# Attention and a gated FFN in one kernel: the second group's units visited two at a time

## The chip, the cores and the metric

The kernel runs on one core of a Trainium2 chip. The metric is the device time of one execution in microseconds. Before the change the median of three runs is 683.46 us (681.92 to 683.64).

## The reference

```python
# q, k, v: 4 batches x 12 heads x 448 tokens x 64, float32
scores = scale * q @ k.T ; upper triangle masked ; attn = softmax(scores)
x = (attn @ v), heads side by side: 1792 tokens x 768
rms = sqrt(mean(x * x) + 1e-6) ; xn = x / rms * rms_g
g = xn @ w_gate ; val = xn @ w_val          # 768 x 1536 each
out = (g * sigmoid(g) * val) @ w_out        # 1536 x 768
```

## The kernel before, in words

**Groups and units.** The tokens are worked in three groups. Groups 0 and 1 hold the first 256 queries of two batches each, group 2 all other queries. Within a group attention is cut into units: a pair of heads of one batch and some of its queries. `UNITS` lists them, `ENDS` = [12, 24, 60] is where each group ends, and `DP` = 3 is the distance in units by which scores run ahead. Units of groups 0 and 1 have `kind` 0: 256 queries in two blocks, 128 queries by 128 keys and 128 queries by 256 keys. Those of group 2 have kind 1 (128 queries, 384 keys) or kind 2 (64 queries of two batches, 448 keys).

**Steps of a unit.** `steps_s(p)` makes the scores of unit p on TensorE (one half e = 0, 1 for each head). VectorE masks and reduces them out of PSUM (L202), ScalarE takes the exponential one slot later (L205), and `norm` (posted seven slots later for kind 0) takes a reciprocal on VectorE (L214) and scales, for units 10 to 23 on ScalarE (L208). `steps_t(p)` gives two steps, one for each e: three transposes on TensorE into a bank and a copy `pt` out of it, for units 12 to 23 on ScalarE (L255). `steps_a(p)` multiplies the copies with v (L275) into a half of one bank and copies the result out (L292, on ScalarE for group 1). The banks of PSUM: `m` two, `s` two, and one each of `t`, `x`, `y` and `a`. Scores of a unit take the two `s` banks; for every second unit of the third group they take `x` and `y`. Transposes of e = 0 go to `t`, those of e = 1 to `x` as far as unit 24, and to `t` after it.

**Order.** It is written out by hand: all engines get their instructions in program order from one Python loop. While group 0's attention runs by itself at first, with a little of the FFN, from then on the FFN of one group runs with the attention of the next beneath it. The FFN of a group is a list of 36 weight units (24 of the gate and value weights, 12 of the output weights); one unit is 18 matmuls of 512 columns, 6 in each of 3 **slots**. After the six matmuls of a slot the loop (L916 to L940) puts in the steps of attention that are due, spread evenly from slot `HOLD` to slot `AT` of the block, then splits and conversions of later weights, and `tick()` runs what was posted with a delay for that slot. So `post(7, f)` means that f's instructions stand at the end of the seventh slot, counted from the one that posts.

```python
while done < goal and (done - at) < (goal - at) * (i - HOLD[w_]) / (AT[w_] - HOLD[w_]):
    steps[done]()
    done += 1
```

In that first block VectorE and ScalarE also convert the 64-bit weights (L414 to L419), split each weight into two parts (L429, L431) and evict every FFN bank (L492 to L505, or L486 in the output part).

**The list of steps.** `round_steps(p)` makes the rounds of groups 0 and 1. For group 1 a round is three steps: `both` (scores of unit p + 3, products of unit p), then the two steps of transposes of unit p + 1. `refill()` stands ahead of group 1's first round: scores of units 12, 13 and 14 and the transposes of unit 12, with empty steps between. `round_of_two(p)` makes the rounds of group 2, four steps for two units: `last` (the last transposes of unit p + 1, then `visit`: loads of v, scores of p + 3 and p + 4, products of p and p + 1, the two copies), and then the transposes of p + 2 (two steps) and the first of p + 3.

Of the kernel before, what the change touches and what calls it, by code (L numbers as in the profile page):

```python
# [34 lines left out]
UNITS = [(g, kind, c, k, NP * (first + k) + c, base + QUERIES[kind] * k)  # L35
         for g, parts in enumerate(GROUPS) for c in range(NP)
         for kind, n, first, base in parts for k in range(n)]
LAST = {(g, c): max(i for i, u in enumerate(UNITS) if u[0] == g and u[2] == c)
        for g in range(NG) for c in range(NP)}
ENDS = [max(i for i, u in enumerate(UNITS) if u[0] == g) + 1 for g in range(NG)]  # L40
# [11 lines left out]
WARM = [9, 0, 0, 2]  # L52
EXTRA = 4
AT = [108, 73]
HOLD = [9, 0]
XT = 768
HX = XT // 2
RING = 6
DP = 3
# [3 lines left out]
def attention_ffn(ctx: ExitStack, tc: tile.TileContext, qk0, qk1, qk2, v, v2, w, g, out, out2):  # L63
# [11 lines left out]
    def pool(name, bufs, at=ctx, **kw):  # L75
        return at.enter_context(tc.tile_pool(name=name, bufs=bufs, **kw))
# [3 lines left out]
    ps = pool("ps", 1, space=PSUM)  # L80
# [13 lines left out]
    def bank(tag, bufs=1):  # L94


        return ps.tile([P, W], F32, tag=tag, name=tag + "_ps", bufs=bufs)
# [34 lines left out]
    def post(delay, fn):  # L132
        if delay <= 0:
            fn()
        else:
            later.setdefault(now[0] + delay, []).append(fn)
# [32 lines left out]
    def blocks(kind):  # L169

        return [(0, P), (P, 2 * P)] if kind == 0 else [(0, KEYS[kind])]

    def steps_s(p):


        if not 0 <= p < len(UNITS):
            return []
        _, kind, _, _, _, _ = UNITS[p]
        pr = hs[p] = dict(norms=[])
        bl = blocks(kind)  # L180
        nb = 2 * len(bl)

        def scores(pss):
            for i, (o, wd) in enumerate(bl):
                for h in range(1 + (kind == 2)):
                    for e in range(2):
                        r = raw_qk[p][e * D: (e + 1) * D, h]
                        if kind == 2:
                            ps, q0, nq = pss[e][h * D: (h + 1) * D, :wd], 0, D
                        else:  # L190
                            ps, q0, nq = pss[e][:, o: o + wd], i * P, P
                        k0 = nq if kind else 2 * P
                        nc.tensor.matmul(ps, r[:, q0: q0 + nq], r[:, k0: k0 + wd],  # L193
                                         start=True, stop=True)

        def softmax(e, i, pss):
            o, wd = bl[i]
            ps, sp = pss[e][:, o: o + wd], pr["sp"][e][:, o: o + wd]
            n = len(bl) * e + i
            nm, sm, rs = (pr[m][:, n: n + 1] for m in ("nm", "sm", "rs"))  # L200
            mk = mask2 if kind == 2 else mask[:, 3 * P - wd:]
            nc.vector.tensor_tensor_reduce(  # L202
                out=sp, in0=ps, in1=mk, scale=nsc, scalar=3.0e38,
                op0=ALU.add, op1=ALU.min, accum_out=nm)
            post(T["exp" if p >= ENDS[0] else "exp0"], lambda: nc.scalar.activation(  # L205
                sp, sp, AF.Exp, bias=nm, scale=-1.0, accum_out=sm))
            if ENDS[0] - 2 <= p < ENDS[1]:
                pr["norms"].append(lambda: nc.scalar.mul(sp, sp, rs))  # L208
            else:
                pr["norms"].append(lambda: nc.gpsimd.tensor_scalar(  # L210
                    sp, sp, rs, 1.0, op0=ALU.mult, op1=ALU.mult))

        def norm():
            nc.vector.reciprocal(pr["rs"][:, :nb], pr["sm"][:, :nb])  # L214
            post(2 if ENDS[0] - 2 <= p < ENDS[0] else 0, lambda: [f() for f in pr["norms"]])

        def step():
            for nm in ("nm", "sm", "rs"):
                pr[nm] = st_p.tile([P, 4], F32, tag=nm, name=nm)
            pr["sp"] = [sp_p.tile([P, S], F32, tag="sp", name="sp") for _ in range(2)]  # L220
            pss = [bank(t_) for t_ in "xy"] if p > ENDS[1] + DP and p % 2 == 0 else [
                bank("s", 2) for _ in range(2)]
            scores(pss)
            for e in range(2):
                for i in range(len(bl)):
                    softmax(e, i, pss)
            post(T["exp" if p >= ENDS[0] else "exp0"], lambda: nc.scalar.activation(
                pr["sm"][:, :nb], pr["sm"][:, :nb], AF.Identity, bias=tiny))
            post(T["norm1" if kind else "norm0"], norm)
            post(2, lambda: load_qk(p + 4))  # L230

        return [step]

    def steps_t(p):

        if not 0 <= p < len(UNITS):
            return []
        _, kind, _, _, _, _ = UNITS[p]
        pr = hs[p]
        kb = KB[kind]  # L240

        def some(e):
            pt = pr["pt", e] = pt_p.tile([P, W], F32, tag=f"pt{e}", name="pt")
            ps = bank("x" if e and p < ENDS[1] + 1 else "t")
            at = 0
            for j in range(NKB[kind]):
                for o, wd in blocks(kind):
                    if kb * j < wd:
                        nc.tensor.transpose(ps[:kb, at: at + P],  # L249
                                            pr["sp"][e][:, o + kb * j: o + kb * (j + 1)], ident)  # L250
                        at += P
            if kind or (e and p < ENDS[0]):
                nc.vector.tensor_copy(pt[:kb, :at], ps[:kb, :at])  # L253
            else:
                nc.scalar.copy(pt[:kb, :at], ps[:kb, :at])  # L255

        return [lambda e=e: some(e) for e in (0, 1)]
# [520 lines left out]
    def round_steps(p):  # L778

        noop = [lambda: None]  # L780
        first = p < ENDS[0]
        s_, ts = (f(n) if not first or n < ENDS[0] else [] for f, n in ((steps_s, p + DP), (steps_t, p + 1)))
        as_ = steps_a(p)

        def products():
            for f in as_:
                f()


        def scores():  # L790
            if p + 2 > 0:
                post(T["lv"], lambda: load_v(p + 2))
            for f in s_:
                f()

        def both():
            scores()
            products()

        ts = (ts + 2 * noop)[:2]  # L800
        return [scores, products, ts[0]] + 2 * noop + ts[1:] if first else [both] + ts

    def refill():

        p, noop = ENDS[0], [lambda: None]
        return (steps_s(p) + 2 * noop + steps_s(p + 1) + noop
                + steps_t(p) + steps_s(p + 2) + noop)

    def round_of_two(p):


        def visit():
            for q in (p, p + 1):
                post(2, lambda q=q: load_v(q + 2))
            for f in steps_s(p + DP) + steps_s(p + DP + 1):
                f()
            fs = steps_a(p), steps_a(p + 1)
            for i in (0, 1):
                for f in fs:
                    f[i]()  # L820

        def transposes(q, i):
            fs = steps_t(q)
            if fs:
                fs[i]()

        def last():
            transposes(p + 1, 1)
            visit()

        return [last] + [lambda q=q, i=i: transposes(q, i) for q, i in ((p + 2, 0), (p + 2, 1), (p + 3, 0))]
# [7 lines left out]
    with tc.manual_schedule():  # L839
# [6 lines left out]
        warm_ps = bank("m", 2)  # L846
        warm(WARM[0])
        steps, ends = [], []
        for p in range(-DP, ENDS[1]):
            steps += round_steps(p)  # L850
            if p + 1 in ENDS:
                ends.append(len(steps))
            if p + 1 == ENDS[0]:
                steps += [lambda: None] * EXTRA + refill()
        steps.append(lambda: steps_t(ENDS[1] + 1)[0]())
        for p in range(ENDS[1], len(UNITS), 2):
            steps += round_of_two(p)
            if p + 2 in ENDS:
                del steps[-3:]
                ends.append(len(steps))  # L860
        done = 0
        n_pre = ends[0] + EXTRA
# [11 lines left out]
        n = 0  # L874
        for t_, s, c in early:
            n = max(n, t_)
# [23 lines left out]
        for s in range(2 * NU):  # L900
            w_ = s // NU
# [2 lines left out]
                xrs.close()  # L904
                side["wrx"] = pool("wrx", 4, ffn1, side="left", reuse_waits="tile")
            if s % NU == 0:
                at, goal = done, ends[w_ + 1] + (w_ == 0)
            if len(LOAD) <= s + 7 < NU:
                post(T["ld"], lambda s=s: load_w(s + 7))
            n = s + 6 - 2 * NU  # L910
# [5 lines left out]
            for k0 in (0, 2, 4):  # L916
# [3 lines left out]
                i = 3 * (s % NU) + k0 // 2 + 1  # L920
                while done < goal and (done - at) < (goal - at) * (i - HOLD[w_]) / (AT[w_] - HOLD[w_]):
                    steps[done]()
# [12 lines left out]
                n = 3 * (s - 2 * NU + 2) + k0 // 2  # L935
# [26 lines left out]
        for v in range(NF):  # L962
            if v % 3 == 1 and v < 9:
                wo_sums(v // 3)
            for i in range(7):
                ps_ = quad_product(v, i)
                quad_result(v, i, ps_)
                if v + 1 < NF:
                    n = (0, 1, None, 2, None, 3, None)[i]
# [7 lines left out]
                if v + 2 < NF:  # L977
                    n = (None, None, 0, 1, None, 2, 3)[i]
# [18 lines left out]
        for q in range(21):  # L997
            i, p = divmod(q, 3)
# [58 lines left out]
```

## Time and profile before

| | |
|---|---|
| median of 3 runs | 683.46 us |
| profiled execution | 683.01 us |
| its span | 681.2 us |
| TensorE busy | 668.9 us (98%) |
| VectorE busy | 533.1 us (78%) |
| ScalarE busy | 378.2 us (56%) |
| GpSimd busy | 301.0 us (44%) |
| granted TensorE clock | 1.00 |

The span is from the first to the last instruction of the profiled execution; the execution's own time has 1.8 us more around it. PE is TensorE's matmuls, PEld its weight loads, DVE VectorE, ACT ScalarE, POOL GpSimd, SP the engine that issues the DMAs. The second group's attention in question runs from about 95 to 235 us of the span.

### The profile page before, as it was taken

The page shows a single profiled execution, that of the slowest core. Times are in us where ns is not written, and L with a number is a line of the kernel's source. Part 1 is how long each engine was busy: PE and PEld are TensorE (multiplying, and loading weights), DVE is VectorE, ACT ScalarE, POOL GpSimd, SP SyncE. Part 2 cuts the span into 40 slices and gives each one's busy share as a digit, 9 for nine tenths or more (in the row PEclk, how much of TensorE's full clock was granted, in tenths as well). Part 3 has the DMA queues.
Part 4 walks back from the last instruction along what each step waited for, and adds up shares of the span by engine and source line. Part 5 has one row for each costly group of instructions (what it writes and reads, how often), then busy time and mean ns, then how long its engine had stood idle before and what let it go on. Part 6 is the DMA issues. An engine that isn't in the chain of part 4 may idle for free. (4 is left out here: it accounts for less than half of the span.)

```text
span 681.2 us, 11945 instructions
## 1 busy us (share of the span) xinstructions
PE 668.9 (98%) x4122; PEld 550.4 (81%) x4122; DVE 533.1 (78%) x1053; ACT 378.2 (56%) x855; POOL 301.0 (44%) x268
## 2 busy tenths in 40 slices
PE   9989999999999999999999999999999999999997
PEld 6566877777777777777777777888999999999997
DVE  4998998999888486777777877387576777779993
ACT  6986779797876444545545453444524342455550
POOL 4971121222235427565765666563353645302220
PEclk9999999999999999999999999999999999999999
DMA  7765788787877456767666645316657474553641
GB/s 256 255 234 199 217 242 298 233 259 233 284 270 279 159 163 228 220 237 211 226 224 222 210 160 179 123 62 206 207 182 252 164 270 172 190 164 83 176 139 63
DMA packets 71357, 138.82 MB, mean 204 GB/s; under 512 B 7744, under 2 KB 39232, under 8 KB 71296
## 3 DMA queue, kind: packets, MB, share of 16 engines
q1 hardware_dynamic: 71296, 138.05, 62.7%
q8 instruction: 33, 0.54, 0.3%
q14 instruction: 28, 0.23, 0.1%
HBM read 104.21 MB, written 33.82 MB: 203 GB/s over the span
## 5 line engine op out<-in xcount | busy, mean ns | idle before, releaser
L210 POOL TENSOR_SCALAR sp<-sp,rs 128x384 f32<-128x384 f32 (+2 forms) x112 | 78.6, 719 | 90.8 <-DVE rs L214 80.3
L475 PE MATMUL m_ps<-xh,w_h 128*128 128x512 f32 x276 | 117.4, 425 | 0.0
L205 ACT ACTIVATE sp<-sp,nm 128x384 f32<-128x384 f32 (+3 forms) x168 | 87.2, 521 | 42.3 <-DVE nm L202 42.3
L477 PE MATMUL m_ps<-xh,w_l 128*128 128x512 f32 x276 | 108.3, 392 | 0.0
L476 PE MATMUL m_ps<-xl,w_h 128*128 128x512 f32 x276 | 108.2, 392 | 0.0
L415 POOL TENSOR_SCALAR w<-w 128x768 f32<-128x768 f32 x36 | 39.2, 1090 | 103.3 <-ACT w_c L414 97.7
L103 POOL TENSOR_TENSOR a_l<-w_q,a_h 128x768 fp32r<-128x768 f32 x24 | 49.5, 2066 | 52.5 <-ACT a_h L516 50.7
L275 PEld LDWEIGHTS a_ps<-pt,v_r 128*64 128x64 f32 (+1 forms) x864 | 41.8, 137 | 31.3 <-issue 9.2
L275 PE MATMUL a_ps<-pt,v_r 128*64 128x128 f32 (+2 forms) x864 | 59.5, 268 | 4.2 <-DVE pt L253 2.8
L103 POOL TENSOR_TENSOR w_l<-w_r,w_h 128x768 fp32r<-128x768 f32 x30 | 59.5, 1991 | 6.2 <-ACT w_h L429 6.0
L477 PEld LDWEIGHTS m_ps<-xh,w_l 128*128 128x128 f32 x276 | 51.9, 188 | 12.0
L475 PEld LDWEIGHTS m_ps<-xh,w_h 128*128 128x128 f32 x276 | 51.9, 188 | 11.8 <-issue 3.7
L253 DVE COPY pt<-t_ps 128x384 f32<-128x384 f32 (+1 forms) x71 | 42.4, 597 | 23.9 <-PE t_ps L249 23.5
L202 DVE CUSTOM_DVE_ANT_0 sp<-s_ps,mask 128x128 f32<-128x128 f32 (+3 forms) x136 | 49.8, 414 | 12.1 <-PE s_ps L193 11.1
L475 PE MATMUL m_ps<-hh,w_h 128*128 128x512 f32 x144 | 58.6, 407 | 0.0
L476 PEld LDWEIGHTS m_ps<-xl,w_h 128*128 128x128 f32 x276 | 52.2, 189 | 7.6
L477 PE MATMUL m_ps<-hh,w_l 128*128 128x512 f32 x144 | 56.2, 391 | 0.0
L476 PE MATMUL m_ps<-hl,w_h 128*128 128x512 f32 x144 | 56.2, 390 | 0.0
L249 PE MATMUL t_ps<-ident,sp 128*128 128x128 f32 (+1 forms) x309 | 50.1, 275 | 0.1
L249 PEld LDWEIGHTS t_ps<-ident,sp 128*128 128x128 f32 (+1 forms) x309 | 37.8, 137 | 14.4 <-issue 2.0
L193 PE MATMUL s_ps<-qk_r 64*128 64x128 f32 (+3 forms) x296 | 42.4, 423 | 0.5 <-DVE nm L202 0.4
L516 ACT CAST a_h<-w_q 128x768 fp32r<-128x768 f32 (+1 forms) x48 | 35.0, 754 | 13.5 <-DMA w_q<-wz 4.2
(196 smaller groups left out, 1677.5 us busy)
## 6 DMA issues: line engine op xcount, KB each, us to landing
w<-in_w SPq DMA_DIRECT2D x36, 768.0 KB, 5.4
w<-w_c SPq DMA_DIRECT2D x36, 384.0 KB, 5.9
w_r<-w SPq DMA_DIRECT2D x36, 384.0 KB, 4.9
qk_r<-in_qk SPq DMA_DIRECT2D x48, 256.0 KB, 4.3
qk_r<-in_qk SPq DMA_DIRECT2D x12, 512.0 KB, 5.6
v_r<-in_v SPq DMA_DIRECT2D x12, 448.0 KB, 4.8
v_r<-in_v SPq DMA_DIRECT2D x24, 192.0 KB, 3.4
wy<-w_r SPq DMA_DIRECT2D x24, 192.0 KB, 4.1
```

What stands on the lines that cost most here:

```text
L103: nc.gpsimd.tensor_tensor(out_, a, b, op=op)
L193: nc.tensor.matmul(ps, r[:, q0: q0 + nq], r[:, k0: k0 + wd], start=True, stop=True)
L202: nc.vector.tensor_tensor_reduce(out=sp, in0=ps, in1=mk, scale=nsc, scalar=3.0e38, op0=ALU.add, op1=ALU.min, accum_out=nm)
L205: post(T["exp" if p >= ENDS[0] else "exp0"], lambda: nc.scalar.activation(sp, sp, AF.Exp, bias=nm, scale=-1.0, accum_out=sm))
L210: pr["norms"].append(lambda: nc.gpsimd.tensor_scalar(sp, sp, rs, 1.0, op0=ALU.mult, op1=ALU.mult))
L249: nc.tensor.transpose(ps[:kb, at: at + P], pr["sp"][e][:, o + kb * j: o + kb * (j + 1)], ident)
L253: nc.vector.tensor_copy(pt[:kb, :at], ps[:kb, :at])
L275: nc.tensor.matmul(av_ps[e * D: (e + 1) * D, p % 2, q0: q0 + n], raw_v[p][:kb, h, j, e, :], pr["pt", e][:kb, a0: a0 + n], start=(j == 0), ...
L415: (T["c1" if s > 4 else "c10"], lambda: nc.gpsimd.tensor_scalar(hf_, hf_, 0.0, 1.0, op0=ALU.mult, op1=ALU.mult)),
L475: nc.tensor.matmul(ps, wh[:, k, :], mh, start=(first and k == ks[0]), stop=False)
L476: nc.tensor.matmul(ps, wh[:, k, :], ml, start=False, stop=False)
L477: nc.tensor.matmul(ps, wl[:, k, :], mh, start=False, stop=(last and k == 5))
```

## The change

The second group gets the third group's rounds. `round_steps` serves group 0 alone. From unit 12 on `round_of_two` makes the rounds: six visits with two units each in place of twelve with one. The scores of every second unit from 16 on go to the banks `x` and `y`. The transposes of e = 1 go to bank `x` only as far as unit 12, and to `t` from unit 13 on. `refill` gets one more step, the first transposes of unit 13. The list for the first FFN block shrinks from 46 steps to 34, and `HOLD` goes from 9 to 12, so its first step stands three slots later.

```diff
-HOLD = [9, 0]
+HOLD = [12, 0]
...
-            pss = [bank(t_) for t_ in "xy"] if p > ENDS[1] + DP and p % 2 == 0 else [
+            pss = [bank(t_) for t_ in "xy"] if p > ENDS[0] + DP and p % 2 == 0 else [
                 bank("s", 2) for _ in range(2)]
...
-            ps = bank("x" if e and p < ENDS[1] + 1 else "t")
+            ps = bank("x" if e and p <= ENDS[0] else "t")
...
-        first = p < ENDS[0]
-        s_, ts = (f(n) if not first or n < ENDS[0] else [] for f, n in ((steps_s, p + DP), (steps_t, p + 1)))
+        s_, ts = (f(n) if n < ENDS[0] else [] for f, n in ((steps_s, p + DP), (steps_t, p + 1)))
...
-        def both():
-            scores()
-            products()
-
         ts = (ts + 2 * noop)[:2]
-        return [scores, products, ts[0]] + 2 * noop + ts[1:] if first else [both] + ts
+        return [scores, products, ts[0]] + 2 * noop + ts[1:]
...
         return (steps_s(p) + 2 * noop + steps_s(p + 1) + noop
-                + steps_t(p) + steps_s(p + 2) + noop)
+                + steps_t(p) + steps_s(p + 2) + noop + [lambda: steps_t(p + 1)[0]()])
...
-        for p in range(-DP, ENDS[1]):
+        for p in range(-DP, ENDS[0]):
             steps += round_steps(p)
-            if p + 1 in ENDS:
-                ends.append(len(steps))
-            if p + 1 == ENDS[0]:
-                steps += [lambda: None] * EXTRA + refill()
-        steps.append(lambda: steps_t(ENDS[1] + 1)[0]())
-        for p in range(ENDS[1], len(UNITS), 2):
+        ends.append(len(steps))
+        steps += [lambda: None] * EXTRA + refill()
+        for p in range(ENDS[0], len(UNITS), 2):
             steps += round_of_two(p)
+            if p + 2 == len(UNITS):
+                del steps[-3:]
             if p + 2 in ENDS:
-                del steps[-3:]
                 ends.append(len(steps))
...
-                at, goal = done, ends[w_ + 1] + (w_ == 0)
+                at, goal = done, ends[w_ + 1]
```

## Rows read from the trace of the kernel before

**Rows 1.** The page's busy time of each engine: us (share of the span) xinstructions.
```profile
PE 668.9 (98%) x4122; PEld 550.4 (81%) x4122; DVE 533.1 (78%) x1053; ACT 378.2 (56%) x855; POOL 301.0 (44%) x268
```

**Rows 2.** Stretches: length, PE, PEld, DVE, ACT, POOL busy; PEclk, DMA share, GB/s.
```profile
95.00:111.00 16.00, 15.83 (x87) 11.70 (x87) 15.84 (x36) 11.90 (x30) 3.74 (x3) 1.00 0.86 275
111.00:130.00 19.00, 19.00 (x102) 14.97 (x102) 16.57 (x28) 16.86 (x44) 3.15 (x3) 1.00 0.78 247
130.00:152.00 22.00, 22.00 (x121) 17.10 (x118) 21.75 (x40) 19.17 (x48) 6.67 (x6) 1.00 0.89 272
152.00:175.00 23.00, 23.00 (x124) 17.75 (x123) 21.74 (x40) 17.92 (x46) 5.30 (x6) 1.00 0.82 243
```

**Rows 3.** Timeline of TensorE, a visit: start, us, engine, line, out<-in, count.
```profile
151.98 0.39 PE L476 MATMUL m_ps<-xl,w_h 128*128 128x512 f32 x1
152.21 0.39 PE L477 MATMUL m_ps<-xh,w_l 128*128 128x512 f32 x1
152.52 0.93 PE L193 MATMUL s_ps<-qk_r 64*128 64x128 f32 x8
153.38 0.87 PE L275 MATMUL a_ps<-pt,v_r 128*64 128x256 f32 x8
154.18 0.50 PE L475 MATMUL m_ps<-xh,w_h 128*128 128x512 f32 x1
154.52 0.40 PE L476 MATMUL m_ps<-xl,w_h 128*128 128x512 f32 x1
```

**Rows 4.** Timeline of TensorE, a step of transposes and the second FFN matmul behind it.
```profile
157.04 0.49 PE L249 MATMUL t_ps<-ident,sp 128*128 128x128 f32 x3
...
157.59 0.39 PE L476 MATMUL m_ps<-xl,w_h 128*128 128x512 f32 x1
```

**Rows 5.** Timeline of TensorE, parts of three visits of the third group.
```profile
238.40 0.49 PE L249 MATMUL t_ps<-ident,sp 128*128 128x128 f32 x3
238.81 0.92 PE L193 MATMUL s_ps<-qk_r 64*128 64x384 f32 x4
...
250.93 1.53 PE L275 MATMUL a_ps<-pt,v_r 128*64 128x128 f32 x24
252.39 0.50 PE L475 MATMUL m_ps<-xh,w_h 128*128 128x512 f32 x1
...
259.91 0.92 PE L193 MATMUL s_ps<-qk_r 64*128 64x384 f32 x4
...
261.40 2.08 PE L275 MATMUL a_ps<-pt,v_r 112*64 112x64 f32 x64
```

**Rows 6.** Timeline of TensorE, two visits' products and the FFN matmul behind them.
```profile
106.63 0.65 PE L275 MATMUL a_ps<-pt,v_r 128*64 128x256 f32 x2
...
108.24 0.50 PE L475 MATMUL m_ps<-xh,w_h 128*128 128x512 f32 x1
...
199.13 0.65 PE L275 MATMUL a_ps<-pt,v_r 128*64 128x256 f32 x2
...
201.09 0.50 PE L475 MATMUL m_ps<-hh,w_h 128*128 128x512 f32 x1
```

**Rows 7.** Timeline of TensorE, the scores of one visit and the transposes behind it.
```profile
95.01 0.93 PE L193 MATMUL s_ps<-qk_r 64*128 64x128 f32 x8
...
99.52 0.49 PE L249 MATMUL t_ps<-ident,sp 128*128 128x128 f32 x3
```

**Rows 8.** Timeline of ScalarE: exponentials, a cast, a copy, and normalisations.
```profile
100.50 0.40 ACT L205 ACTIVATE sp<-sp,nm 128x128 f32<-128x128 f32 x1 [2.37 <-DVE nm L202]
...
102.61 0.82 ACT L429 CAST w_h<-w_c 128x768 fp32r<-128x768 f32 x1
...
104.65 0.48 ACT L255 COPY pt<-t_ps 128x384 f32<-128x384 f32 x1
...
110.69 1.50 ACT L208 ACTIVATE sp<-sp,rs 128x128 f32<-128x128 f32 x4 [1.50 <-DVE rs L214]
```

**Rows 9.** Timeline of VectorE, the first reduce of the scores of 95.01.
```profile
100.18 0.28 DVE L202 CUSTOM_DVE_ANT_0 sp<-s_ps,mask 128x128 f32<-128x128 f32 x1
```

## The prediction

> **What bounds the kernel now.** I read the engines' busy shares first. TensorE is busy 98% of the span [rows 1], so what counts is what a change takes from or adds to TensorE's own stream. The change touches only the first block of the FFN (36 weight units), under which the second group of attention runs, some 95 to 235 us into the span. So I read the table of stretches there next. From 95 to 175 us TensorE is busy 79.8 of 80 us, and VectorE 15.84 + 16.57 + 21.75 + 21.74 = 75.9 of 80 us, 95% [rows 2]. The reader is to see two nearly full engines: TensorE sets the end, and VectorE would be full if TensorE became some 5% faster. Last I read TensorE's order of instructions and, beside it, ScalarE's and VectorE's.
>
> A step of the FFN is one matmul per 0.23 us (151.98 to 152.21 [rows 3]), so a slot, six of them, is 1.39 us. The block's loop puts step n of a list (from 0) into the first slot i with n < N (i - H) / (108 - H). Now N = 46 and H = 9: twelve visits, six or seven slots apart, in slots 29 to 100. After, N = 34 and H = 12: visits in slots 41, 52, 63, 75, 86 and 97.
>
> **What the change removes on TensorE.** A single visit (scores of a unit, products of another) runs from the last FFN matmul before it at 152.21 to the second one after it at 154.52 [rows 3]: 2.31 us, less the two FFN steps in it (0.46) = 1.85 us. Of this 0.86 is scores, 0.80 products, 0.08 and 0.11 the way in and out. A step of transposes (three) costs 157.04 to 157.59 less one FFN step [rows 4] = 0.32 us. Two units cost 2 x 1.85 + 4 x 0.32 = 4.98 us now.
>
> A pair has three steps of transposes alone (0.96) and one visit in which the fourth stands first. The third group's visits price it [rows 5]: transposes and the way into the scores 0.41 (238.40 to 238.81), the scores of two units of one form 1.49 (259.91 to 261.40; those have 384 columns, as here 128 + 256), products of two units 1.46 with 384 columns each (250.93 to 252.39), the way out 0.11 as above. That is 3.47, with the other three steps 4.43 us. The pair saves 0.55 us, six pairs **3.3 us**. Bounds: if only the doors were saved (0.08 + 0.11 of a visit, 0.08 of a transposes' step), 0.27 x 6 = 1.6; if the way from transposes into scores (0.17) came to the 0.08 of a single visit, 3.8. I take the rows' 3.3, since it is these forms of instruction.
>
> **Stalls that go.** Two of the twelve visits wait for the copied transposes of e = 1, which ScalarE brings late: from the first product to the next FFN matmul 108.24 - 106.63 = 1.61 us and 201.09 - 199.13 = 1.96 us, against 0.80 in the undisturbed visit [rows 3, 6]. That is 0.81 + 1.16 = **2.0 us** which these visits lose. In the new order product p has its transposes copied long before; for p + 1 see below. Together 5.3 us could go.
>
> **What is late next.** Three things get shorter notice, and all hang on ScalarE and VectorE, which work behind TensorE: the scores made at 95.01 are reduced by VectorE from 100.18 and their exponentials run from 100.50 to 102.61; the transposes of 99.52 are copied from 104.65 to 105.13, so 5.6 us after they began; the scores of 95.01 are normalised from 110.69 [rows 7 to 9].
> (1) Both transposes of a unit use one bank. The next step of transposes must wait until the copy has read it; it comes three slots later (3 x 1.39 + 0.32 = 4.5 us), at two places (units 14 and 17) two slots later (3.1 us). Behind the waiting transposes stands TensorE's whole stream.
> (2) The last transposes of unit p + 1 stand in the visit that multiplies with them: 0.41 + 1.49 + 0.73 = 2.6 us from their start to the first use, where now at least two slots lie between.
> (3) The first transposes of unit p + 3 come 8 or 9 slots after its scores: 3.06 (the visit from the scores on) + 0.64 + 8 x 1.39 = 14.8 us, or 16.2. In the trace the first two of the four normalisations are done 110.69 + 0.75 - 95.01 = 16.4 us after the scores. Now there are some 15 slots between.
> The loads don't bind: the queue takes q, k and v two at once every 11 slots, and the buffers (4 and 3) are free two slots after the visit. The other steps are moved, not changed: the first by three slots, which costs nothing as the FFN's matmuls fill the time, and the last visit ends three slots earlier.
>
> **What these waits cost.** Unhindered, the same work of 95 to 175 us (seven visits, a stall of 0.81) would take 80 - 3.5 x 0.55 - 0.8 = 77.3 us, in which VectorE has its 75.9 us of work: 98%. Its 4.1 us of idleness now are waits for ScalarE in the middle of its order, which pairs don't take away. If it keeps them, this stretch stays at 80 us, and 2.7 us are given back, whichever of (1) to (3) or the evictions of the FFN's banks TensorE feels it by. The ends are 0 (VectorE runs at 98%) and some 6 (it falls to 92%, because two units' reduces and exponentials come in one burst); I take **2.7**, the share that the row shows. In the later part (five visits, units with lighter evictions) the saving is 2.5 x 0.55 + 1.16 = 2.5 us. There I walked ScalarE's order for one pair: exponentials of two units take 2 x 2.1 us [rows 8] and begin some 4 us after the visit's start, so they end near 8.3; with two or three casts behind them (104.65 - 102.61 = 2.0 [rows 8]) the copy of the next transposes ends near 11, and the transposes after them come at 10.7 where the first gap is two slots and at 12.1 where it is three: a wait of some 0.4 at the one place (unit 20) and none at the others. The first normalisations end near 15.9, where an 8-slot gap gives 14.8 to 15.2: 0.4 to 1 us. I take **1.4 us** for this part, with ends 0 and 3.
>
> Sum: -3.3 - 2.0 + 2.7 + 1.4 = -1.2 us. The profiled execution took 683.01 us (span 681.2 and 1.8 around it): 681.8. The median of the runs shown is 0.45 above that execution, so as a median **682.3 us**.
>
> A rule speaks against the change. The Trainium skill, Perfetto Trace Analysis, section Matmuls, asks that independent groups of matmuls rotate through different banks, so that the emptying of one overlaps the next group. By it, the second bank for the transposes is worth having; the trace agrees so far as its copies end 5.6 us after the transposes began [rows 7, 8], longer than the new gap of 4.5. What that would make of the time is the second rival.
>
> **Rivals.** (A) *The whole gain.* VectorE's idle 4.1 us shrink since TensorE hurries it less unevenly, and stalls stay under 1.5 us in all: 683.0 - 5.3 + 1 = 678.7, as a median 679. For it: no FFN matmul waits for an eviction anywhere in this stretch, so VectorE's lateness has some reserve; the new order has fewer units in the first half (six visited by slot 72, now seven). Against it: rows 2.
> (B) *The single bank decides; slower.* The copies stay as late as now. Each unit's second transposes then wait 5.6 - 4.5 = 1.1 us, eleven times 12 us, against 5.3: 690; with the copies 0.4 us earlier it is 685.5. The point from which it decides is a copy ending 5.0 us after its transposes began: 11 x 0.5 eats the gain. For it: the copy stands in ScalarE's order behind the exponentials, and two units' of them come at once. Against it: each wait of TensorE lets ScalarE and VectorE catch up, so the waits do not add up in full, and by the walk above copies end 3.7 us after.
> (C) *No pairing gain.* The pairs save only the doors (1.6) and the stalls come back in other places: 683.5 to 685. For it only that the third group's units have one block and not two.
>
> **How the numbers follow.** A measurement of this kernel tells about 0.3% from no change, 2 us. Forecast (680.8 to 684.0 as a median) 0.45; A, or most of it (677.7 to 680.8) 0.25; C and the milder side of B (684 to 685.5) 0.10; B (above 685.5) 0.20. Faster by over 0.3% means below 681.4: all of A and a quarter of the forecast, 0.36. Slower means above 685.5: 0.20, with a little of C 0.22. Within: 0.42. The range holds the forecast, most of A, C, and the lower half of B: 678.2 to 687.5.
>
> **What would show it.** In the trace after: six visits in this stretch, the merged one 3.5 us from its transposes to the second FFN matmul (if 3.9 or more without a wait, the price of pairs was wrong); TensorE's waits for the copies, for the normalised rows and for the bank together near 4 us, most of them before unit 24 of the FFN; VectorE's busy share from the first visit to unit 24 near 95% (at 98%, A holds). Waits of about 1 us at each second step of transposes would show B. The third group and all behind it should run as before, only shifted; if the time changes there, the forecast is wrong in kind.

## The result, and the profile after

The changed kernel takes 687.28 us (median of 4 runs, 687.04 to 689.93), the kernel before 682.69 beside it: ratio 1.0072, 95% interval 1.0056 to 1.0088. It is slower by 4.6 us, where 682.3 was forecast. The profiled execution took 687.25 us, its span 685.3, against 683.01 and 681.2.

The loss lies ahead of the third group. The transposes that open that group's first visit began at 238.40 us before [rows 5] and begin at 242.49 after, 4.1 us later; from there to the end of the span both need 442.8 us. First the page's busy times and the two stretches (columns as in [rows 1, 2]).

```profile
PE 667.5 (97%) x4122; PEld 551.0 (80%) x4122; DVE 537.0 (78%) x1053; ACT 379.1 (55%) x855; POOL 300.6 (44%) x268
```
```profile
95.00:175.00 80.00, 75.80 (x400) 58.22 (x399) 73.67 (x138) 64.86 (x160) 19.94 (x17) 1.00 0.80 256
175.00:235.00 60.00, 58.01 (x309) 44.53 (x309) 49.73 (x87) 44.66 (x106) 20.79 (x18) 1.00 0.73 244
```
From 95 to 175 us TensorE is now idle for 4.2 of 80 us, where it was 0.2 [rows 2]. VectorE, with nearly the same work, is busy 92% and no longer 95%: no engine is full any more, so they wait for each other.

Next TensorE's own order: start, duration, engine, line, out<-in, count, and in brackets the idle time before and what ended it.
```profile
113.17 0.39 PE L477 MATMUL m_ps<-xh,w_l 128*128 128x512 f32 x1
113.41 0.49 PE L249 MATMUL t_ps<-ident,sp 128*128 128x128 f32 x3
...
115.33 1.30 PE L275 MATMUL a_ps<-pt,v_r 128*64 128x256 f32 x10
117.77 0.86 PE L275 MATMUL a_ps<-pt,v_r 128*64 128x256 f32 x6 [1.14 <-ACT pt L255]
118.57 0.50 PE L475 MATMUL m_ps<-xh,w_h 128*128 128x512 f32 x1
...
155.85 0.39 PE L477 MATMUL m_ps<-xh,w_l 128*128 128x512 f32 x1
157.54 0.55 PE L249 MATMUL t_ps<-ident,sp 128*128 128x128 f32 x3 [1.30 <-ACT pt L255]
...
160.98 0.50 PE L475 MATMUL m_ps<-xh,w_h 128*128 128x512 f32 x1
...
178.50 0.39 PE L477 MATMUL m_ps<-hh,w_l 128*128 128x512 f32 x1
178.72 0.49 PE L249 MATMUL t_ps<-ident,sp 128*128 128x128 f32 x3
179.14 0.93 PE L193 MATMUL s_ps<-qk_r 64*128 64x128 f32 x8
...
180.65 1.52 PE L275 MATMUL a_ps<-pt,v_r 128*64 128x256 f32 x16
182.11 0.50 PE L475 MATMUL m_ps<-hh,w_h 128*128 128x512 f32 x1
182.44 0.39 PE L476 MATMUL m_ps<-hl,w_h 128*128 128x512 f32 x1
...
214.16 0.39 PE L477 MATMUL m_ps<-hh,w_l 128*128 128x512 f32 x1
215.91 0.84 PE L249 MATMUL t_ps<-ident,sp 128*128 128x128 f32 x3 [1.37 <-ACT sp L208]
216.50 0.48 PE L475 MATMUL m_ps<-hh,w_h 128*128 128x512 f32 x1
```
The visit at 178.50 waits for nothing: 182.44 - 178.50 less two FFN steps (0.46) = 3.48 us, forecast 3.47. From FFN matmul to FFN matmul it is 182.11 - 178.50 = 3.61. A wait's price is read against that, by starts: the visit of units 12 and 13 takes 118.57 - 113.17 = 5.40, so it loses 1.79, although the bracket says 1.14 idle. The rest is overlap that the wait breaks: an FFN matmul is drawn 0.39 us long and the next one starts 0.23 after it (151.98 and 152.21 [rows 3]), so a bracket, which counts from the drawn end, comes out too short. The same subtraction gives 1.52 at 155.85 and, against the 0.47 of an unstalled step of transposes, 1.87 at 214.16.

So measured, all waits of the stretch lose 9.8 us:

| TensorE waits for | where | us |
|---|---|---|
| the single bank (1) | step of transposes at 126.5, visits at 135.9 and 155.9, step at 190.1 | 0.65 + 0.17 + 1.52 + 0.77 = 3.1 |
| copies that the visit's products need (2) | visit at 113.2 | 1.8 |
| normalised rows (3) | third step of transposes behind the visits at 113 and 199 | 0.70 + 1.87 = 2.6 |
| evictions of the FFN's banks | 104.4 and 109.6, ahead of the first visit | 0.75 + 0.80 = 1.55 |
| small ones, four | three of them in third steps of transposes too | 0.8 |

The waits view names the releasers (us in all, times, longest; it counts idle time alone).
```profile
PE t_ps L249 <- ACT pt L255: 2.3, 3, 1.3
PE a_ps L275 <- ACT pt L255: 1.6, 3, 1.1
PE t_ps L249 <- ACT sp L208: 1.6, 2, 1.4
...
PE m_ps L475 <- DVE t_sb L502: 0.6, 1, 0.6
PE m_ps L475 <- DVE gr L492: 0.5, 1, 0.5
```
The sum: -3.3 for the pairs, -2.0 for the two old stalls, +9.8 = +4.5; the start of the third group's first visit says +4.1. The other 0.4 is not assigned.

The largest wait of each of the three kinds has one source. Rows of ScalarE's order, then of VectorE's:
```profile
110.98 0.48 ACT L255 COPY pt<-t_ps 128x384 f32<-128x384 f32 x1
113.81 1.50 ACT L208 ACTIVATE sp<-sp,rs 128x128 f32<-128x128 f32 x4 [2.36 <-DVE rs L214]
115.21 0.62 ACT L493 ACTIVATE t_sb<-gr 128x512 f32<-128x512 f32 x1
...
117.27 0.46 ACT L255 COPY pt<-t_ps 128x384 f32<-128x384 f32 x1
...
152.19 2.89 ACT L208 ACTIVATE sp<-sp,rs 128x128 f32<-128x128 f32 x8 [1.36 <-DVE rs L214]
...
157.02 0.46 ACT L255 COPY pt<-t_ps 128x384 f32<-128x384 f32 x1
...
215.46 1.49 ACT L208 ACTIVATE sp<-sp,rs 128x128 f32<-128x128 f32 x4 [3.14 <-DVE rs L214]
```
```profile
112.74 0.95 DVE L431 TENSOR_TENSOR w_l<-w_c,w_h 128x768 fp32r<-128x768 f32 x1
113.60 0.17 DVE L214 RECIPROCAL rs<-sm 128x4 f32<-128x4 f32 x1
...
158.97 0.29 DVE L202 CUSTOM_DVE_ANT_0 sp<-s_ps,mask 128x128 f32<-128x128 f32 x1 [1.58 <-PE s_ps L193]
...
211.85 1.62 DVE L417 SCALAR_TENSOR_TENSOR w<-w 128x768 int32<-128x768 int32 x1 [0.20 <-POOL w L415]
...
215.25 0.17 DVE L214 RECIPROCAL rs<-sm 128x4 f32<-128x4 f32 x1
```
The normalisations of unit 14 stand at the head of ScalarE's queue from 111.4 on, idle for 2.36 us, since VectorE reaches the reciprocal only at 113.60. (Two of VectorE's instructions ahead of it, 1.66 us at 108.16 and 1.43 at 110.34, run beside GpSimd's L415 and take 0.95 elsewhere: 1.2 us of its lateness; see the last section.) Behind them stand three pieces of FFN work and the copy at 117.27, for which the products at 117.77 wait. A reciprocal of 0.17 us holds up ScalarE, and ScalarE holds up TensorE. At 152.19 it is the same with eight normalisations: the copy that empties the bank comes at 157.02, and TensorE waits for it until 157.54. At 215 the queue's head, after 3.14 us, holds up TensorE directly, which wants the rows themselves. And it goes round: VectorE then waits 1.58 us, until 158.97, for scores that the stalled TensorE brings late. By the waits view of 95 to 175 us VectorE waited 3.0 us for ScalarE before; after, it waits 3.9 for ScalarE and these 1.6 for TensorE.

### The profile page after: what moved, and what is told of

Same layout as the page of the kernel before. It is cut to its first block, busy times and chain, and to the rows that moved or that the text cites. A ratio compares the mean times of both kernels' runs of the same rounds, so it can differ in the third digit from the quotient of the medians.

```text
span 685.3 us, 11937 instructions
## 1 busy us (share of the span) xinstructions
PE 667.5 (97%) x4122; PEld 551.0 (80%) x4122; DVE 537.0 (78%) x1053; ACT 379.1 (55%) x855; POOL 300.6 (44%) x268
## 5 line engine op out<-in xcount | busy, mean ns | idle before, releaser
L210 POOL TENSOR_SCALAR sp<-sp,rs 128x384 f32<-128x384 f32 (+2 forms) x112 | 76.7, 703 | 97.0 <-DVE rs L214 80.7
L415 POOL TENSOR_SCALAR w<-w 128x768 f32<-128x768 f32 x36 | 40.5, 1128 | 109.4 <-ACT w_c L414 92.9
L275 PE MATMUL a_ps<-pt,v_r 128*64 128x128 f32 (+2 forms) x864 | 57.4, 267 | 4.7 <-DVE pt L253 2.4
L249 PE MATMUL t_ps<-ident,sp 128*128 128x128 f32 (+1 forms) x345 | 57.3, 276 | 4.1 <-ACT pt L255 2.3
L249 PEld LDWEIGHTS t_ps<-ident,sp 128*128 128x128 f32 (+1 forms) x345 | 41.9, 138 | 22.6 <-ACT pt L255 3.9
L202 DVE CUSTOM_DVE_ANT_0 sp<-s_ps,mask 128x128 f32<-128x128 f32 (+2 forms) x116 | 43.0, 419 | 11.1 <-PE s_ps L193 10.1
L431 DVE TENSOR_TENSOR w_l<-w_c,w_h 128x768 fp32r<-128x768 f32 x36 | 41.1, 1140 | 4.9 <-ACT w_h L429 4.9
```

Source lines behind the costliest of these rows:

```text
L202: nc.vector.tensor_tensor_reduce(out=sp, in0=ps, in1=mk, scale=nsc, scalar=3.0e38, op0=ALU.add, op1=ALU.min, accum_out=nm)
L210: pr["norms"].append(lambda: nc.gpsimd.tensor_scalar(sp, sp, rs, 1.0, op0=ALU.mult, op1=ALU.mult))
L249: nc.tensor.transpose(ps[:kb, at: at + P], pr["sp"][e][:, o + kb * j: o + kb * (j + 1)], ident)
L275: nc.tensor.matmul(av_ps[e * D: (e + 1) * D, p % 2, q0: q0 + n], raw_v[p][:kb, h, j, e, :], pr["pt", e][:kb, a0: a0 + n], start=(j == 0), ...
L431: post(T[("wl0", "wl0", "wl2", "wl2", "wl4")[s] if s < 5 else "wl"], lambda: nc.vector.tensor_tensor(l, t, f32(h), op=ALU.subtract))
```

## The experiments

The kernel before was run beside each batch: 682.3, 682.5, 682.6 and 682.6 us. Intervals are of the ratio to it.

**Is it the single bank, and is it the late start?** Transposes of the changed kernel that rotate over three banks:

```diff
-            ps = bank("x" if e and p <= ENDS[0] else "t")
+            ps = bank("tx" [e] if p <= ENDS[0] else "t" if p >= ENDS[1] else ("tx", "yt")[p % 2][e])
```


> The new order, but the transposes of units 13 to 23 rotate through three banks (even units: t, x; odd units: y, t), so no step of transposes meets a bank that is still to be read. In the trace of the new order the waits for that bank are 1.53 + 0.76 + 0.64 = 2.9 us. Theory (VectorE late, ScalarE's order held up by it; every wait of TensorE is one face of that): the wait moves on in part, the time comes down by 0.5 to 2 us, 685.3 to 686.8. Rival (the single bank is the cause): all 2.9 us or more come back, 684.4 or below.

686.95 us, 1.0065 (1.0052 to 1.0078): 0.3 us less than the change, too little to tell from nothing. It is just above the theory's 685.3 to 686.8 and far from the rival's 684.4 or less. The bank's waits are gone, but in the waits view those for rows took their place:
```profile
PE y_ps L249 <- ACT sp L208: 2.7, 3, 1.4
```
The same steps of transposes now wait at the next door, for the normalised rows: TensorE is ready for the first of them 0.8 us earlier than in the change, while the reciprocal comes at 130.59 and not at 130.71. In this order the bank does not decide by itself.

The changed kernel with its first step three slots earlier, as before:

```diff
-HOLD = [12, 0]
+HOLD = [9, 0]
```


> The new order with the first step three slots earlier, HOLD 9 as before the change. The new trace has two waits of an FFN matmul for VectorE's eviction (0.67 and 0.72 us) ahead of the first visit, where the old one has none. Theory (VectorE is full whatever the order): these two waits go or move, within 1.5 us of 687.3. Rival (the late start crowds the stretch): 2 us or more faster, 685.3 or below.

690.37 us, 1.0112 (1.0091 to 1.0133). Both sides missed. The evictions' waits went, so they did belong to the late start; but waits for rows rose to five, which lose 0.9 to 2.2 us each. Given the pairs, the late start is worth 3 us.

Each of the two alone in the old order, one visit a unit:

```diff
-            ps = bank("x" if e and p < ENDS[1] + 1 else "t")
+            ps = bank("x" if e and p <= ENDS[0] else "t")
```


> The old order (single visits) with one part of the change alone: transposes of e = 1 of group 1 in bank t from unit 13 on. Copies end 2 to 6.8 us after their transposes began, the next step comes 3.1 or 4.5 us after. Adding up the old trace's lateness, about 10 steps would wait some 1 us each. Theory: waits let ScalarE catch up, 2 to 4 us slower than before, 685 to 687. Rival (the bank is the cause by itself): 5 us or more slower, 688 or above. If it is within 1 us of before, the bank does nothing in single visits.

690.83 us, 1.0128 (1.0111 to 1.0145): the rival's side, above 688. In the old order the bank does decide: giving it up costs 8.5 us. Its waits view shows three waits where before has none of this kind:
```profile
PE t_ps L249 <- ACT pt L255: 5.6, 3, 2.5
```
The profiled execution took 687.41 us at a granted clock of 1.000; the others took 690 to 692 at 0.993 to 0.995 (last section), so at the full clock it is 5.1 us, in one execution.

```diff
-HOLD = [9, 0]
+HOLD = [12, 0]
```


> The old order with the other small part of the change alone, HOLD 12. Theory: the attention is packed into 96 slots and not 99, and the FFN alone runs longer at VectorE's pace; 0 to 1.5 us slower than before, 682.7 to 684.2. Rival (the late start is what costs): 2 us or more slower.

686.87 us, 1.0062 (1.0050 to 1.0075), the rival's side: three slots cost 4.6 us in the old order. The visits' waits for copies, 1.2 us in the kernel before and 0.5 at most, are 2.6 with one of 1.6:
```profile
PE a_ps L275 <- ACT pt L255: 2.6, 3, 1.6
```
So neither "costs nothing" nor a fixed price holds: the start shifts which work meets which, and its sign depends on the order.

**Is it VectorE's lateness?** The step L417 of the weights' conversion left out of both kernels, so that L419 takes the high word alone:

```diff
-            (at2, lambda: nc.vector.scalar_tensor_tensor(
-                out=lo, in0=lo, scalar=29, in1=hi, op0=ALU.logical_shift_right, op1=ALU.bitwise_or)),
...
-                out=ti, in0=ti, scalar=3, in1=lo, op0=ALU.logical_shift_left, op1=ALU.bitwise_or)),
+                out=ti, in0=ti, scalar=3, in1=hi, op0=ALU.logical_shift_left, op1=ALU.bitwise_or)),
```
The change:

> The new order with VectorE relieved: the step of L417 (0.95 us a unit, 36 units) is left out, so the last three bits of each weight's mantissa are missing and the rest of the conversion stays. VectorE goes from some 97% to some 75% busy in the first FFN block. Theory (VectorE nearly full and 3 to 5 us late; its lateness reaches TensorE through ScalarE's order): the 9.8 us of waits fall below 4, 679.5 to 682.5, so level with or below the relieved old order. Rival (short notice alone; ScalarE's queue is late by itself): waits stay at 6 us or more, 684 or above, and 3 us or more above the relieved old order.

The kernel before:

> The old order with the same step of VectorE left out (the same three bits missing). Theory: only its 2 us of waits in visits can go, 680 to 682.5. Rival: the old order, too, is held by VectorE all along, 679 or below.

679.86 us, 0.9957 (0.9945 to 0.9970), and 680.38 us, 0.9969 (0.9958 to 0.9981), both where the theory had them. The 4.6 us between the two orders is gone, and the new one is level or a little ahead (0.5 us; the intervals overlap). The first stretch, new order and then old:
```profile
95.00:175.00 80.00, 79.54 (x447) 63.04 (x446) 57.45 (x139) 66.17 (x163) 20.17 (x17) 1.00 0.82 266
```
```profile
95.00:175.00 80.00, 80.00 (x434) 61.59 (x432) 57.03 (x126) 65.91 (x161) 20.93 (x18) 1.00 0.84 259
```
With VectorE at 72% TensorE waits 0.5 us in this stretch and not 4.2, with the same bank, the same order and the same start. About 2.6 us of lost time remain, most of it for bank and rows in the later part.

**Do the normalisations carry it?** First moved from ScalarE to GpSimd for units 13 to 23 of the change:

```diff
-            if ENDS[0] - 2 <= p < ENDS[1]:
+            if ENDS[0] - 2 <= p <= ENDS[0]:
```


> The new order, with the normalisations of units 13 to 23 on GpSimd in place of ScalarE. In the new trace ScalarE stands idle 10.4 us at the head of its order for the reciprocals (5 times), with the copies of transposes behind. Theory: with that out of ScalarE's order copies come sooner, but GpSimd's part of the conversion now waits behind the normalisations, and VectorE behind that: 684 to 688, the waits moved again. Rival (ScalarE's order alone is the bottleneck): 3 us or more faster than the new order, 684 or below.

696.34 us, 1.0207 (1.0189 to 1.0225). Missed by both: four of them take GpSimd 3.73 to 4.86 us (ScalarE 1.50), eight take it 5.34 to 6.31 (ScalarE 2.88), and TensorE waits for the rows eight times (8.9 us). It tells nothing of ScalarE's queue. Then left out:

```diff
-                pr["norms"].append(lambda: nc.scalar.mul(sp, sp, rs))
+                p <= ENDS[0] and pr["norms"].append(lambda: nc.scalar.mul(sp, sp, rs))
```
The change:

> The new order without the normalisations of units 13 to 23 (the reciprocals stay; these rows are left unnormalised). It takes 2.8 us a pair off ScalarE, its waits for reciprocals, and the transposes' wait for normalised rows (3.1 us in the new trace). Theory: these 3.1 go, and most of the waits behind ScalarE's waiting head (1.8 in the first visit, 1.5 at unit 17) go with them: 681.5 to 684. Rival (VectorE's fullness alone sets the pace of this stretch, whatever ScalarE does): less than 2 us gained, 685.3 or above.

The kernel before:

> The old order without the normalisations of units 13 to 23 (their rows are left unnormalised; the reciprocals stay). Counterpart to the new order without them (682.46 us, 4.8 below the new order). Theory (the normalisations in ScalarE's order, waiting for a late VectorE, hurt only where notice is short): the old order has 15 slots between scores and transposes and gains 2 us at most, 680.3 to 682.5, so that both orders come out level. Rival (ScalarE is simply overloaded in either order): 3 us or more gained, 679.3 or below.

682.46 us, 0.9995 (0.9986 to 1.0004), and 681.43 us, 0.9978 (0.9968 to 0.9989). Both lie in the theory's ranges. The new order gains 4.8 us by it, the old one 1.2. So 3.6 of the 4.6 us hang on the normalisations, though these two runs do not part their work from their waiting; what the new order keeps is waits for the bank (1.4 and 0.8 us at two steps), the first visit's 0.65 and the evictions' 1.4.

**VectorE relieved in another way.** Every third split of a weight (L431) from unit 8 on GpSimd, in both kernels:

```diff
-            if s < NU or s > NU + 2 * NF and s % 2:
+            if s < NU and not (s > 5 and s % 3 == 2) or s > NU + 2 * NF and s % 2:
```
The change:

> The new order with VectorE relieved without leaving work out: of the weights' low parts (L431, 0.95 us each) every third one from unit 8 on goes to GpSimd, as in the second FFN block. That takes 0.3 us of 4.6 a unit from VectorE. Theory (VectorE's fullness is the root): 2 to 5 us faster than the new order, 682.3 to 685.3. Rival (GpSimd's 2 us operations slow VectorE and the conversion behind them as much as they relieve it): 686.5 or above.

The kernel before:

> The old order with the same third of the low parts on GpSimd. Theory: at most its 2 us of waits can go, 680.4 to 682.8. Rival: 684 or above, since GpSimd's operations hold up VectorE.

691.91 us, 1.0136 (1.0116 to 1.0156), and 685.91 us, 1.0041 (1.0024 to 1.0058): both are slower, as the rival had it. The split takes GpSimd some 2 us, and VectorE's instructions beside it get longer. VectorE's rows in the first of these two, with such a split on GpSimd from 110.89 to 113.43:
```profile
107.04 0.96 DVE L419 SCALAR_TENSOR_TENSOR w_c<-w_c,w 128x768 int32<-128x768 int32 x1
...
111.82 2.42 DVE L419 SCALAR_TENSOR_TENSOR w_c<-w_c,w 128x768 int32<-128x768 int32 x1
114.16 0.17 DVE L214 RECIPROCAL rs<-sm 128x4 f32<-128x4 f32 x1
```
2.42 us for what takes 0.96, and the reciprocal stands behind it: here VectorE was not relieved.

**Where the normalisations stand.** Five slots after the scores and not seven, units 13 to 23 of the change:

```diff
-            post(T["norm1" if kind else "norm0"], norm)
+            post(5 if ENDS[0] < p < ENDS[1] else T["norm1" if kind else "norm0"], norm)
```


> The new order with the normalisations of units 13 to 23 posted five slots after the scores and not seven, so two slots more notice ahead of the transposes that need them. In the new trace these transposes wait 3.1 us. Theory (reciprocals and exponentials are late by themselves; the earlier normalisation makes ScalarE stand at its head for longer, with copies behind): the wait moves, 685.8 to 688.5. Rival (the two slots are what is missing): 684.8 or below.

684.75 us, 1.0028 (1.0018 to 1.0039): 2.5 us less than the change, the rival's side, if by a hair; the theory, at 685.8 or above, missed. No wait for rows is left, and now the bank's have grown:
```profile
PE t_ps L249 <- ACT pt L255: 3.5, 4, 1.2
```
This mirrors the rotating banks: with one short notice lengthened, TensorE waits at the other.

So both edits together, rotating banks and five slots:

> The new order with both: normalisations of units 13 to 23 posted after five slots, and transposes rotating through three banks. Theory now (two short notices one behind the other; each alone hides the other): the 3.5 us of waits for the bank left in the run with early normalisations go too, 680.5 to 682.8, level with before or a little faster. Rival (VectorE's fullness keeps its price; the wait moves to a third place, the evictions or the products): 683.5 or above.

681.27 us (11 runs), 0.9983 (0.9973 to 0.9994): as the theory had it, and 6.0 us less than the change, where the two alone give 0.3 and 2.5, and 1.3 less than the kernel before. The gain is smaller than the 0.3% named ahead, but with this many runs the interval lies below one.
```profile
95.00:175.00 80.00, 78.52 (x414) 61.39 (x413) 75.89 (x140) 66.83 (x164) 20.22 (x18) 1.00 0.83 266
175.00:235.00 60.00, 60.00 (x324) 47.08 (x323) 51.87 (x89) 43.65 (x100) 22.14 (x20) 1.00 0.73 246
```
The later stretch has no wait at all. In ScalarE's order the normalisations now stand ahead of both copies, and not between them:
```profile
110.15 1.50 ACT L208 ACTIVATE sp<-sp,rs 128x128 f32<-128x128 f32 x4 [1.05 <-DVE rs L214]
111.55 0.61 ACT L503 CAST hh<-t_sb 128x512 fp32r<-128x512 f32 x1
112.06 0.47 ACT L255 COPY pt<-y_ps 128x384 f32<-128x384 f32 x1
113.53 0.63 ACT L493 ACTIVATE t_sb<-gr 128x512 f32<-128x512 f32 x1 [1.01 <-DVE gr L492]
...
115.61 0.46 ACT L255 COPY pt<-t_ps 128x384 f32<-128x384 f32 x1
```
The second copy is through at 116.07 and not at 117.73. What remains are the evictions ahead of the first visit (0.70 + 0.74) and three visits that lose 0.53, 1.01 and 0.63. Three neighbours bound this version. Five slots in the old order:

> The old order with the normalisations two slots earlier. Theory: transposes come some 15 slots after the scores there, so rows are never late; only ScalarE's order shifts: 681.5 to 684. Rival (early normalisation helps ScalarE's order by itself): 681 or below.

684.55 us, 1.0035 (1.0023 to 1.0047): worse by 2, a little above the 684 expected; there the visits lose 1.94, 0.85 and 0.85 to late copies. The early normalisation is no gain of its own; it belongs to the pairs. Four slots:

```diff
-            post(5 if ENDS[0] < p < ENDS[1] else T["norm1" if kind else "norm0"], norm)
+            post(4 if ENDS[0] < p < ENDS[1] else T["norm1" if kind else "norm0"], norm)
```


> As the run with both, the normalisations after four slots. Theory: five slots were enough for the rows; at four ScalarE and VectorE stand longer for the exponentials of two units, within 1 us of the run with five, rather slower. Rival (rows are still short): 1 us or more faster than with five.

684.58 us, 1.0033 (1.0020 to 1.0046), 3.3 us worse than five, which neither side had: the waits of products for copies are back (2.9 us, one of 2.1). And five slots with `HOLD` 9:

> As the run with both, with the first step three slots earlier (HOLD 9). Without the two repairs this start was 3 us slower than HOLD 12. Theory (that price was paid in the same two notices): it falls to 1 us or less, 680.5 to 683.5. Rival (it is the start itself): again 2 us or more slower than the run with both at HOLD 12.

682.61 us, 1.0004 (0.9993 to 1.0015): the late start is worth 1.3 us here, a little above the theory's 1 us, and not 3.

## Why the prediction was wrong

**Right.** The price of a pair: the unstalled visit takes 3.48 us (forecast 3.47), and no extra cost of the form was found; rival C falls. The two old stalls are gone. The third group runs as before, 4.1 us later. The three short notices named are the places where TensorE waits, the bank, the visit's own copies and the rows (7.5 of the 9.8 us), and 6.7 of the 9.8 us fall before 175 us, where most were expected.

**The step that failed** is "What these waits cost": "I take 2.7, the share that the row shows", and 1.4 for the later part, 4.1 in all. Measured: 6.7 us from 95 to 175, 2.8 later and 0.3 ahead, 9.8 in all. The step assumed that VectorE keeps its 95%. It fell to 92% (73.67 of 80), which the text had as its far end, "some 6 (it falls to 92%)". (By its own working 92% gives 75.9 / 0.92 - 77.3 = 5.2, not 6; the 6.7 measured lie beyond both.) With 6 and 3, the text's own far ends, the sum is +3.7 us, near the 4.1 measured. So the mechanism was seen and the size chosen from the wrong end: an engine's busy share in the old order is no floor for its share in a new one, because VectorE waits in turn for a TensorE that is stalled. The text took all 4.1 us of VectorE's old idleness as waits for ScalarE; the waits view shows 3.0. Where VectorE does keep its 95%, in the run with both edits (75.89 of 80), TensorE loses 3.6 us in this stretch and nothing in the later one, near the 4.1 forecast; the notices are longer there, so this shows the size and not the reason.

**What the walk of ScalarE's order left out.** It priced copies and rows by ScalarE's own work in the later part (ends near 11 and 15.9 us after a visit). It found the one place where the bank is short there, unit 20 (0.4 us forecast, 0.77 measured at 190.1), and gave the rows 0.4 to 1 us, where 1.87 was lost at 214.16. In the rows of after ScalarE stands idle at the head of its queue, 2.36 and 3.14 us, for a reciprocal which VectorE reaches late. Three ways of touching that link support it: leaving out the VectorE step brings the two orders level, leaving out the normalisations takes away 3.6 of the 4.6 us, and moving them two slots forward with the banks rotated takes away 6.0.

**"The other steps are moved, not changed: the first by three slots, which costs nothing as the FFN's matmuls fill the time."** This failed too. Those matmuls need VectorE's evictions, and two of them wait, 1.55 us; with `HOLD` 9 these waits go. The prediction named such evictions only among the ways in which VectorE's lateness could be felt. In the old order the same three slots cost 4.6 us; with the pairs they save 3. That sign was nowhere in the prediction.

**Rival B**, the single bank, has a time near the measured one (its range began at 685.5) but is not the cause as told: four steps waited, not eleven, and rotating the banks alone gave 0.3 us. By the rule cited there, that groups of matmuls should rotate through banks (the Trainium skill, Perfetto Trace Analysis, section Matmuls), the second bank is worth having; the runs agree in the old order, where giving it up cost 5.1 us at the full clock and 8.5 as a median, and in the new one only once the rows are early too: then it is 684.75 - 681.27 = 3.5 us. Rival A needed VectorE to be hurried without waiting more; with both edits 2.3 of its 5.3 us are there when the third group's first visit begins (238.40 against 236.13).

**Open.** That profiled run loses some of it after 236 us (its span is only 0.7 shorter than before); it is one run, 1.0 us above its median, and was not followed. Why three slots of start fall so differently in the two orders is shown only by which waits appear, not derived. Rotated banks and the early start together, with the normalisations left at seven slots, were not run, so what these two parts cost jointly in the new order stays open.

## What to carry to other kernels

When two engines are nearly full and pass work through a third one's in-order queue, price a rearrangement by who stands at the head of that queue and for whom; when that is the late engine, give the far end of the range its weight, which here was the nearer one. Short notices in series hide each other: removing one or the other showed 0.3 and 2.5 us, removing both 6.0, so a fix that fails alone is tried again with its neighbour. Lost time is read from starts of the steady work around a wait, not from the idle time in brackets (1.79 against 1.14 us here).

## What the runs showed of the hardware

TensorE's clock fell behind some long waits. In the change with `HOLD` 9, two stretches, and TensorE's rows there:
```profile
192.00:196.00 4.00, 2.24 (x11) 1.46 (x10) 3.88 (x7) 1.71 (x6) 0.00 (x0) 0.99 0.39 68
196.00:199.30 3.30, 3.30 (x10) 2.56 (x9) 1.18 (x2) 3.30 (x8) 0.44 (x1) 0.50 0.97 330
```
```profile
194.75 0.84 PE L249 MATMUL t_ps<-ident,sp 128*128 128x128 f32 x3 [1.69 <-ACT sp L208]
...
195.66 0.40 PE L476 MATMUL m_ps<-hl,w_h 128*128 128x512 f32 x1
...
198.82 0.63 PE L475 MATMUL m_ps<-hh,w_h 128*128 128x512 f32 x1
199.25 0.45 PE L476 MATMUL m_ps<-hl,w_h 128*128 128x512 f32 x1
```
TensorE had been busy 2.24 of 4.00 us; then for 3.3 us the granted clock was 0.50, the 1.2 GHz level, and an FFN step took 0.43 us and not 0.23. That wait cost its own 2.2 us and then 1.5 more (199.25 - 195.66 = 3.59 us for nine steps, which at 0.23 are 2.07). The run with normalisations after four slots shows it again: TensorE busy 1.78 of 3.90 us from 136.00 on (one wait of 2.12), then 0.50 from 139.90 to 141.80. But the change itself shows no such fall behind its idle 1.37 us at 215.9 (clock 1.00 in its stretches), and the profile of the old order with one bank none behind an idle 2.45 us, with TensorE busy 1.05 of 3.50 us from 102.00 on. What tells the cases apart is not shown here. In the old order with one bank the executions at a lower mean clock were the longer ones: 687.41 us at 1.000, 690 to 692 at 0.993 to 0.995. So a wait can be dearer than its own length, and need not be, which no step of the prediction had.

A second surprise is VectorE beside GpSimd: 2.42 us for an instruction that takes 0.96 alone. It was there in the kernel before: L431 takes 1.65 us at 119.97, while GpSimd runs L415 from 119.45 to 120.80, and 0.95 at 136.11 with GpSimd idle.
